# A gated S4 convolution and GLU kernel: products over 64 rows in three of its transform stages

## The chip, the cores and the metric

The kernel runs on one core of one Trainium2 chip. The core has five engines, each with its own instruction list that it works off in order: TensorE (PE, matrix products; its weight loads are shown apart as PEld), VectorE (DVE), ScalarE (ACT), GpSimd (POOL) and SyncE (SP), which here issues all DMA transfers. Transfers are carried out by 16 DMA engines. Engines wait for each other through semaphores. The metric is the time of one execution on the device in microseconds (us).

## The reference

Inputs are u of 2048 positions x 512 channels and the parameters of two branches. What is computed, cut to what matters:

```python
dt = exp(log_dt)[:, None]
P = exp((dt * A)[:, :, None] * l[None, None, :])      # A complex, 512 channels x 128 states
K = einsum("dn,dnl,dn->dl", Cc, P, dt * Bc).real      # one kernel of 2048 taps per channel
y = irfft(rfft(pad(u)) * rfft(pad(K)))[:L] + u * Dskip  # causal convolution per channel
b = (sigmoid(u @ w_gate) * (u @ w_up)) @ w_down       # GLU, inner width 1792
g = sigmoid((u * gate_w).sum(-1, keepdims=True))
out = g * y + (1 - g) * b
```

All inputs and outputs are fp32.

## The kernel before

**Two streams of work.** One stream is the GLU (`glu`), whose products use fp32 values split into a rounded high part and a low part (type fp32r): three products for each block of 128 rows, one pass of TensorE each. `hidden` (L416) makes 24 such products into the tiles `gups`, two PSUM buffers at a time out of a tag `gu` with three; the down projection (L367) adds 9 or 12 into `dps`. Altogether there are 1344 + 672 = 2016 GLU products of 128 x 128 x 512. The other stream is the convolution, done as a transform of length 2048 = 32 x 64 in plain fp32. An fp32 product leaves two records in the profile, since TensorE passes over it twice.

**The convolution's stages.**

- `rows` (L382): for each of 16 row blocks of u, the 32-point stage as two row-tiled products (each 64 rows of the array x 128 columns, at row positions 0 and 64, into two PSUM buffers), written to the DRAM tensor `a_u`.
- `kgen` (L192): for each of 16 groups of 32 channels, DVE builds powers by doubling (`double`, L181; three operations per step), TensorE forms K's taps (`kps`, L221: 64 products of 32 columns each), ACT copies them to `kst`, and TensorE applies the 32-point stage (L231): 16 products with all 128 rows of `kst` as weights and `wk` moving. `wk` has 128 columns; it is block diagonal, four blocks of 32 rows, so three quarters of it are zeros. ACT copies the results into `kev` (L235); after each four groups two transfers of 1 MB write it to `a_k`.
- `finish` (L251): for each of 16 q (two of the 32 frequencies k each) it loads the constants `w_in` and `wv` and the data `au` and `ak`, applies the 64-point stage to both (`stage2`, L243: column-tiled products of 64 columns at column positions 0 and 64), multiplies the spectra on DVE (L267, L268, four operations), and combines them to real part (L273) and imaginary part (L274). Three ACT copies of 64 partitions (L275 to L277) then move the parts so that each of the two k has its real part in partitions 0 to 63 and its imaginary part in 64 to 127. Two full products (L280, tile `ips`, one PSUM buffer, tag `kg`) do the inverse 64-point stage, ACT evicts them (L282), and each goes to the DRAM tensor `b_s`, laid out as [128 = (position, re/im)] x 32 k x 512.
- `final` (L313): for each of 16 row blocks m, one transfer of 512 KB brings `b_in` in, two column-tiled products with `wf` (128 rows x 64 columns, of which half are zeros) do the inverse 32-point stage, DVE adds the GLU's part (L322), and the result is written to `out`.

**What sets the order.** The program text interleaves the streams: `run_b(n)` advances the GLU by n units at each step of `kgen`, `finish` and `final` (ROW, MID, END, LAST set how much). From that text a planner makes, at build time, one fixed instruction list per engine: it takes instructions by priority as its own model says that their inputs and buffers are ready. `kgen`'s TensorE part runs at high priority. The chip then follows these lists whatever the real durations are. So an edit of one stage can move instructions of all others. A buffer is shared by all tiles of one tag; a tile waits until the one that had the buffer has been read for the last time. The tag `big` (three buffers of 512 KB) holds `au` and `ak` in `finish` and `b_in` in `final`; `fft` (two PSUM buffers) holds the outputs of L231, L247, L319 and L390; `o` (two buffers) the results on their way out. The pool `mid` (`rows`, `kgen`) is given up before the pool `end` (`finish`, `final`) is filled, so the first loads of `finish` follow the last `a_k` transfer.

**The stages' place in time.** `rows` and `kgen` come first, then `finish`, then, since every output row needs all 32 k, `final` behind the last write of `b_s`.

Of the kernel before, what the change touches and what calls it, by code (L numbers as in the profile page):

```python
# [25 lines left out]
OP = mybir.AluOpType  # L26
# [20 lines left out]
def constants():  # L47
# [5 lines left out]
    wk = np.zeros((4, 32, 2, 4, 32))  # L53
    wf = np.zeros((2, 2, 32, 2, 32))
    for j in range(2):
        for c in range(2):
            for jp in range(2):
                wu[jp, j, :, jp, c, j, :] = fwd[c]
            wf[j, c, :, j, :] = fwd[c].T / L
    for j in range(4):  # L60
        for c in range(2):
            wk[j, :, c, j, :] = fwd[c]
# [3 lines left out]
    for k in range(32):  # L66
# [6 lines left out]
    wv = wv.reshape(16, 2, P, P).transpose(0, 2, 1, 3)  # L73
# [3 lines left out]
        "c_wu": f(wu, P, 2, P), "c_wf": f(wf, P, 64), "c_wk": f(wk, P, 2, P),  # L77
# [5 lines left out]
def body(ctx, tc, xp, xt, prm, ldt, dsk, gw, wgu, wdn, c_wu, c_wf, c_wk, c_w2, c_wv, c_pw, out):  # L83
# [7 lines left out]
    b_s = dr.tile([P, 32, D], F32, name="b_s")  # L91
# [13 lines left out]
    wk = cst.tile([P, 2, P], F32, name="wk")  # L105
# [86 lines left out]
    def kgen(pp):  # L192
        nxt = bases(pp, 0)
        for gi in range(NG):
# [31 lines left out]
            kv = [k[:, :, 32 * s4:32 * s4 + 32].rearrange("p k (j s) -> p s j k", j=4) for k in kev]  # L226
            for s in range(0, 8, 4):
                p = fps()
                for i in range(4):
                    for c in range(2):  # L230
                        mm(p[64 * c:64 * c + 64, P * i:P * i + P], kst[:, s + i], wk[:, c], start=True, stop=True,  # L231
                           tile_position=(0, 64 * c), skip_group_check=True)
# [18 lines left out]
    def finish(pp):  # L251
        for q in range(16):
# [18 lines left out]

            y = pp.tile([P, 2, D], F32, name="y", bufs=2)
            nc.vector.tensor_tensor(y[:, 0], t1[:, 0], t1[:, 1], op=OP.subtract)  # L273
            nc.vector.tensor_tensor(t2[:, 0], t2[:, 0], t2[:, 1], op=OP.add)  # L274
            nc.scalar.activation(y[:64, 1], y[64:, 0], AF.Copy)  # L275
            nc.scalar.activation(y[64:, 1], t2[64:, 0], AF.Copy)
            nc.scalar.activation(y[64:, 0], t2[:64, 0], AF.Copy)  # L277
            for kb in range(2):
                p = ps.tile([P, D], F32, tag="kg", name="ips")
                mm(p, wv[:, kb], y[:, kb], start=True, stop=True)  # L280
                ev = pp.tile([P, D], F32, name="evb", bufs=3)
                nc.scalar.activation(ev, p, AF.Copy)  # L282
# [30 lines left out]
    def final(pp, wf, m):  # L313

        b = pp.tile([P, 2, D], F32, tag="big", bufs=3, name="b_in")
        nc.sync.dma_start(b, b_s[8 * m:8 * m + 8].rearrange("(j r) k d -> (r k) j d", j=2))
# [214 lines left out]
```

## Time and profile before

| | |
|---|---|
| median of the runs (758.28 to 763.95) | 760.19 us |
| the profiled execution, time | 766.59 us |
| its span | 764.7 us |
| granted TensorE clock, mean over the span | 0.966 |
| PE busy | 709.3 us (93%) |
| DVE busy | 622.5 us (81%) |
| ACT busy | 379.6 us (50%) |
| DMA, mean rate | 161 GB/s, 123.03 MB in all |
| first product of `finish` | at 572.5 us |
| last product of the inverse stage (L280) starts | at 714.9 us |
| first product of `final` (L319) | at 722.5 us |

Times inside the profile count from the start of the span. Busy time is the union of an engine's instructions; a matmul's end is modelled, so TensorE shown as busy is not TensorE at its peak. "gups<-xh,gu" reads: writes tile gups, reads xh and gu; "x32" counts records. A view of windows gives busy time in stretches; the chain gives the work that ended last, followed back from the end, each piece with its start and length; SPq rows are SP issuing a transfer or waiting to.

### The profile page before, as it was taken

Reading aid. Unit: us, or ns where it says so; the run is one execution under the profiler, and the core shown is the slowest. Engines: PE = TensorE matmul, PEld = TensorE weight load, DVE = VectorE, ACT = ScalarE, POOL = GpSimd, SP = SyncE. Lnnn points to the kernel's source line nnn. Section 1 sums busy time; section 2 is a strip of 40 time slices with the busy share of each in tenths; the row PEclk is TensorE's granted clock in tenths of the full one; section 3 lists DMA queues with packets and bytes.
Section 4 is the critical chain, followed back from the end, with each engine's and each line's share of the span. In section 5 each row is a group of like instructions: output and inputs, shape, how many; then the busy total and the mean of one; then the engine's idle time right before and its main releaser. Section 6 shows DMA issues by size and latency. Waiting matters only on the chain.

```text
span 764.7 us, 12698 instructions
## 1 busy us (share of the span) xinstructions
PE 709.3 (93%) x5024; PEld 478.7 (63%) x5024; DVE 622.5 (81%) x851; ACT 379.6 (50%) x624; POOL 3.6 (0%) x36
## 2 busy tenths in 40 slices
PE   5978869999999999999899998999999999999994
PEld 3445437787878778877687786877873333333640
DVE  5889796989998999998999898999927576477452
ACT  5264536381845446374565734637135655656310
POOL 0000000000000000000000000000000000000000
PEclk9789959999999999999999999999999999999998
DMA  6667652353134033655014330423167787876497
GB/s 230 185 201 215 171 158 77 128 188 132 63 110 140 34 132 109 220 172 188 12 34 157 122 150 8 138 96 99 56 244 255 266 264 240 266 249 227 143 308 249
DMA packets 63323, 123.03 MB, mean 161 GB/s; under 512 B 8480, under 2 KB 23072, under 8 KB 62240
## 3 DMA queue, kind: packets, MB, share of 16 engines
q1 hardware_dynamic: 63264, 122.23, 48.6%
q8 instruction: 39, 0.64, 0.3%
q14 instruction: 20, 0.16, 0.1%
HBM read 79.74 MB, written 42.47 MB: 160 GB/s over the span
## 4 chain that ended last, share of the span: by engine, by line
PE 44%; DVE 24%; ACT 14%; DMA 12%; issue 5%; SPq 1%; DVEq 0%; ACTq 0%
PE gups L424 13%; PE dps L367 11%; PE fps L247 8%; DVE T L189 5%; DVE T L190 5%; DVE tmp L188 4%; DMA wst<-wgu 4%; PE ips L280 4%; PE kps L221 3%; ACT L431 2%; PE fps L390 2%; DMA b_in<-b_s 2%; PE fps L231 2%; ACT gu L404 2%; DVE h L432 2%
## 5 line engine op out<-in xcount | busy, mean ns | idle before, releaser
L424 PE MATMUL gups<-xh,gu 128*128 128x512 f32 x896 | 294.5, 404 | 12.7 <-ACT gu L404 10.3
L424 PEld LDWEIGHTS gups<-xh,gu 128*128 128x128 f32 x896 | 170.6, 192 | 66.0 <-issue 12.9
L424 PE MATMUL gups<-xl,gu 128*128 128x512 f32 x448 | 181.3, 405 | 0.0
L367 PE MATMUL dps<-dnw,hh 128*128 128x512 f32 x448 | 152.9, 406 | 11.2 <-ACT hh L433 11.2
L188 DVE TENSOR_TENSOR tmp<-T,bz 128x64 f32<-128x64 f32 (+2 forms) x96 | 114.8, 1196 | 2.4
L190 DVE TENSOR_TENSOR T<-T,tmp 128x64 f32<-128x64 f32 (+2 forms) x96 | 114.7, 1195 | 0.8
L367 PEld LDWEIGHTS dps<-dnw,hh 128*128 128x128 f32 x448 | 84.3, 191 | 49.6 <-ACT hh L433 16.9
L189 DVE TENSOR_TENSOR T<-T,bz 128x64 f32<-128x64 f32 (+2 forms) x96 | 114.7, 1195 | 0.0
L424 PEld LDWEIGHTS gups<-xl,gu 128*128 128x128 f32 x448 | 86.2, 192 | 28.2 <-issue 10.5
L367 PE MATMUL dps<-dnw,hl 128*128 128x512 f32 x224 | 90.1, 404 | 2.1 <-DVE hl L434 1.3
L433 ACT ACTIVATE hh<-h 128x512 fp32r<-128x512 f32 x56 | 35.1, 628 | 70.1 <-DVE h L432 70.1
L431 ACT ACTIVATE sg<-gups 128x512 f32<-128x512 f32 x56 | 33.4, 596 | 50.5 <-PE gups L424 50.1
L367 PEld LDWEIGHTS dps<-dnw,hl 128*128 128x128 f32 x224 | 42.9, 192 | 15.8 <-issue 4.2
L432 DVE TENSOR_TENSOR h<-gups,sg 128x512 f32<-128x512 f32 x56 | 38.2, 685 | 16.9 <-PE gups L424 14.3
L404 ACT ACTIVATE gu<-wst 128x1024 fp32r<-128x1024 f32 x28 | 29.6, 1058 | 41.8 <-DMA wst<-wgu 29.2
L267 DVE TENSOR_TENSOR t<-fps,uf 128x512 f32<-128x512 f32 x32 | 22.0, 687 | 31.2 <-PE fps L247 19.8
L434 DVE TENSOR_TENSOR hl<-h,hh 128x512 fp32r<-128x512 f32 x56 | 38.4, 687 | 9.4 <-ACT hh L433 9.2
L247 PE MATMUL fps<-ak,w_in 128*64 128x512 f32 x128 | 42.1, 610 | 0.1
L235 ACT ACTIVATE kev<-fps 128x256 f32<-128x256 f32 x64 | 33.7, 675 | 15.3 <-PE fps L231 15.3
L247 PE MATMUL fps<-au,w_in 128*64 128x512 f32 x128 | 38.4, 610 | 1.9 <-DVE ud L301 0.8
L373 DVE TENSOR_TENSOR acc<-acc,dps 128x512 f32<-128x512 f32 x48 | 32.2, 682 | 7.8 <-PE dps L367 7.7
L221 PEld LDWEIGHTS kps<-T 128*32 128x32 f32 x2048 | 31.6, 115 | 8.8 <-issue 8.8
(84 smaller groups left out, 691.1 us busy)
## 6 DMA issues: line engine op xcount, KB each, us to landing
wst<-wgu SPq DMA_DIRECT2D x28, 512.0 KB, 4.4
a_u<-evu SPq DMA_DIRECT2D x32, 256.0 KB, 3.3
a_k<-kev SPq DMA_DIRECT2D x8, 1024.0 KB, 6.1
au<-a_u SPq DMA_DIRECT2D x16, 512.0 KB, 5.6
ak<-a_k SPq DMA_DIRECT2D x16, 512.0 KB, 5.0
b_s<-evb SPq DMA_DIRECT2D x32, 256.0 KB, 2.5
b_in<-b_s SPq DMA_DIRECT2D x16, 512.0 KB, 4.7
wsd<-wdn SPq DMA_DIRECT2D x28, 256.0 KB, 3.3
```

The source lines that it names most:

```text
L188: nc.vector.tensor_tensor(t2, src, sb, op=OP.mult)
L189: nc.vector.tensor_tensor(dst, src, br, op=OP.mult)
L190: nc.vector.tensor_tensor(dst, dst, t2[:, :, ::-1], op=OP.add)
L221: mm(p[32 * j:32 * j + 32, s].rearrange("p (a b) -> p a b", a=2), T[:, 0, ch, c], T[:, 1:3, ch, c], start=(c == 0), stop=(c == 1), tile_po ...
L247: mm(p[64 * kb:64 * kb + 64], w[:, kb, 64 * c:64 * c + 64], a(kb), start=True, stop=True, tile_position=(0, 64 * kb), skip_group_check=True)
L367: mm(p, a[:, hs], dnw[:, b], start=(n == 0), stop=(n == last))
L404: nc.scalar.activation(gu[:, 0], s4, AF.Copy)
L424: mm(p, gu[:, a, k, dc], b[:, dc], start=(n == 0), stop=(n == 11))
L431: nc.scalar.activation(sg, pp[0], AF.Sigmoid)
L432: nc.vector.tensor_tensor(h, pp[1], sg, op=OP.mult)
L433: nc.scalar.activation(hh, h, AF.Copy)
L434: nc.vector.tensor_tensor(hl, h, hh.bitcast(F32), op=OP.subtract)
```

## The change

Three stages are rewritten, and the DRAM layout between two of them.

- **K's first stage.** The constant `wk` keeps two of its four blocks (64 columns). The 128 rows of `kst` are taken as two halves of 64 rows; each of 8 s x 2 halves x 2 parts (re, im) is a product of 64 rows x 64 columns at one of four tile positions, 64 columns moving. 32 products per group replace 16; both PSUM buffers of `fft` are taken at once, one per half.
- **The inverse 64-point stage.** `y` keeps real and imaginary parts where DVE leaves them (the imaginary part is written to `y[:, 1]`). The three ACT copies go. Each k is one half of the rows; its result is the sum of two products of 64 rows (re, then im) accumulated in its own PSUM buffer, one of tag `kg` and one of tag `gu`. Four products replace two.
- **The last stage.** `b_s` becomes [64 positions][32 k][2 parts][512]. `final` runs once per pair of row blocks (called at odd m). It takes two `big` buffers, each filled by two transfers of 256 KB, one per row block into its own half of the partitions. Eight products of 64 rows x 32 columns fill two PSUM buffers, one per row block; `wf` loses its zeros. Then come both results and both writes.

```diff
-            kv = [k[:, :, 32 * s4:32 * s4 + 32].rearrange("p k (j s) -> p s j k", j=4) for k in kev]
-            for s in range(0, 8, 4):
-                p = fps()
-                for i in range(4):
+            ph = [fps(), fps()]
+            for s in range(8):
+                for jh in range(2):
+                    r = slice(64 * jh, 64 * jh + 64)
                     for c in range(2):
-                        mm(p[64 * c:64 * c + 64, P * i:P * i + P], kst[:, s + i], wk[:, c], start=True, stop=True,
-                           tile_position=(0, 64 * c), skip_group_check=True)
-                p4 = p.rearrange("p (s j k) -> p s j k", s=4, j=4)
+                        mm(ph[jh][64 * c:64 * c + 64, 64 * s:64 * s + 64], kst[r, s], wk[r, c], start=True, stop=True,
+                           tile_position=(64 * jh, 64 * c), skip_group_check=True)
+            for jh in range(2):
+                p4 = ph[jh].rearrange("p (s j k) -> p s j k", s=8, j=2)
                 for i in range(2):
-                    nc.scalar.activation(kv[i][:, s:s + 4], p4[:, :, :, 16 * i:16 * i + 16], AF.Copy)
+                    kv = kev[i][:, :, 32 * s4 + 16 * jh:32 * s4 + 16 * jh + 16].rearrange("p k (j s) -> p s j k", j=2)
+                    nc.scalar.activation(kv, p4[:, :, :, 16 * i:16 * i + 16], AF.Copy)
...
-            nc.vector.tensor_tensor(t2[:, 0], t2[:, 0], t2[:, 1], op=OP.add)
-            nc.scalar.activation(y[:64, 1], y[64:, 0], AF.Copy)
-            nc.scalar.activation(y[64:, 1], t2[64:, 0], AF.Copy)
-            nc.scalar.activation(y[64:, 0], t2[:64, 0], AF.Copy)
+            nc.vector.tensor_tensor(y[:, 1], t2[:, 0], t2[:, 1], op=OP.add)
+
+            pi = [ps.tile([P, D], F32, tag="kg", name="ips"), ps.tile([P, D], F32, tag="gu", bufs=3, name="ips")]
+            for c in range(2):
+                for kb in range(2):
+                    r = slice(64 * kb, 64 * kb + 64)
+                    mm(pi[kb], wv[r, c], y[r, c], start=(c == 0), stop=(c == 1), tile_position=(64 * kb, 0))
             for kb in range(2):
-                p = ps.tile([P, D], F32, tag="kg", name="ips")
-                mm(p, wv[:, kb], y[:, kb], start=True, stop=True)
                 ev = pp.tile([P, D], F32, name="evb", bufs=3)
-                nc.scalar.activation(ev, p, AF.Copy)
+                nc.scalar.activation(ev, pi[kb], AF.Copy)
                 nc.sync.dma_start(b_s[:, 2 * q + kb], ev)
...
-        b = pp.tile([P, 2, D], F32, tag="big", bufs=3, name="b_in")
-        nc.sync.dma_start(b, b_s[8 * m:8 * m + 8].rearrange("(j r) k d -> (r k) j d", j=2))
-        p = fps()
-        for j in range(2):
-            mm(p[64 * j:64 * j + 64], wf, b[:, j], start=True, stop=True, tile_position=(0, 64 * j),
-               skip_group_check=True)
-        o = pp.tile([P, D], F32, tag="o", bufs=2, name="o")
-        nc.vector.scalar_tensor_tensor(o, p, g[:, m:m + 1], accs[m], op0=OP.mult, op1=OP.add)
-        nc.sync.dma_start(out[m], o)
+        ph = [fps(), fps()]
+        for h in range(2):
+            b = pp.tile([P, 2, D], F32, tag="big", bufs=3, name="b_in")
+            for jb in range(2):
+                l2 = 4 * (m + jb) + 2 * h
+                nc.sync.dma_start(b[64 * jb:64 * jb + 64], b_s[l2:l2 + 2].rearrange("x k c d -> (k c) x d"))
+            for x in range(2):
+                for jb in range(2):
+                    r, o = slice(64 * jb, 64 * jb + 64), 64 * h + 32 * x
+                    mm(ph[jb][o:o + 32], wf[r], b[r, x], start=True, stop=True, tile_position=(64 * jb, o),
+                       skip_group_check=True)
+        for jb in range(2):
+            o = pp.tile([P, D], F32, tag="o", bufs=2, name="o")
+            nc.vector.scalar_tensor_tensor(o, ph[jb], g[:, m + jb:m + jb + 1], accs[m + jb], op0=OP.mult, op1=OP.add)
+            nc.sync.dma_start(out[m + jb], o)
...
-            final(pp, wf, m)
+            if m % 2:
+                final(pp, wf, m - 1)
             run_b(LAST * left)
```

The constants follow (`wk` with 64 moving columns, `wf` with 32, `wv` in the order of parts and halves), and `b_s` is declared as `[64, 32, 2, D]`.

More of the change, by code (lines that the diff above doesn't have):

```diff
@@ L52, in constants @@
     wu = np.zeros((2, 2, 32, 2, 2, 2, 32))
-    wk = np.zeros((4, 32, 2, 4, 32))
-    wf = np.zeros((2, 2, 32, 2, 32))
+    wk = np.zeros((2, 2, 32, 2, 2, 32))
+    wf = np.tile(fwd.transpose(2, 0, 1), (2, 1, 1, 1)) / L
     for j in range(2):
@@ L58, in constants @@
                 wu[jp, j, :, jp, c, j, :] = fwd[c]
[L59 to L62, printed above, removed]
+            wk[:, j, :, c, j, :] = fwd[c]
     l2, k2 = np.arange(64)[:, None], np.arange(64)[None, :]
@@ L90, in body @@
     a_k = dr.tile([NQ, P, 32, P], F32, name="a_k")
-    b_s = dr.tile([P, 32, D], F32, name="b_s")
+    b_s = dr.tile([64, 32, 2, D], F32, name="b_s")
     dts = dr.tile([16, 32], F32, name="dts")
```

8 lines of the change are left out of this document (4 added, 4 removed).

## The prediction

> **What bounds the kernel now.** I read four views: busy time by windows, the chain that ended last, SP's own timeline, and the groups by shape.
>
> ```profile
> 200.00:300.00 100.00, 98.58 (x852) 80.42 (x841) 96.31 (x124) 50.57 (x78) 0.65 (x6) 1.00 0.31 108
> 300.00:400.00 100.00, 96.20 (x835) 77.62 (x835) 92.34 (x116) 56.37 (x89) 0.63 (x6) 0.98 0.37 124
> 650.00:700.00 50.00, 50.00 (x156) 16.66 (x155) 30.86 (x55) 28.84 (x54) 0.00 (x0) 1.00 0.79 256
> 745.00:750.00 5.00, 2.16 (x8) 0.46 (x8) 2.13 (x4) 0.00 (x0) 0.00 (x0) 1.00 0.96 324
> 750.00:755.00 5.00, 1.54 (x4) 0.54 (x6) 0.95 (x2) 0.00 (x0) 0.00 (x0) 0.81 0.93 322
> ```
>
> After the window come busy us of PE, weight loads, DVE, ACT and POOL, then clock, DMA share and GB/s. There are three stages. While K is generated, DVE is busy 92 to 96%; PE's 96 to 98% there flatters it, because ends are modelled. In `finish` PE never pauses and DVE is at 62%. At the end PE is below half and the DMA engines are 93 to 96% busy. So a PE gain is worth little in the first stage, all of itself in the second, and nothing in the third. The chain gives the borders and the durations:
>
> ```profile
> 555.33 1.90 PE fps L231 x32
> 557.22 5.67 PE gups L424 x24
> 562.89 8.45 PE dps L367 x36
> 571.34 0.68 PE gups L424 x3
> ...
> 572.47 3.83 PE fps L247 x16
> ...
> 714.56 0.90 PE ips L280 x2
> ...
> 716.10 2.49 DMA b_s<-evb
> ...
> 718.66 3.65 DMA b_in<-b_s
> ...
> 722.45 1.08 PE fps L319 x4
> 723.53 0.89 PE gups L424 x3
> 724.42 1.01 PE fps L319 x4
> ...
> 742.80 3.56 DMA b_in<-b_s
> ```
>
> One GLU product (L424, L367) costs 8.45/36 = 0.235 us. The last K stage ends at 557.2. The first `finish` product starts at 572.5, because a_k has to be written and au and ak loaded first; 63 GLU products fill that hole. The last inverse product ends at 715.5, so `finish` takes 143.0 us. The first `final` product starts 7.0 us later, the last GLU product ends at 742.8, and the rest up to 764.7, 21.9 us, is transfers.
>
> **The change, part by part.** Prices first.
>
> ```profile
> 46.70 1.11 PE fps L390 x4
> 622.15 1.87 PE fps L247 x8
> 650.68 1.01 PE fps L247 x4
> 654.02 0.86 PE ips L280 x2
> 584.06 0.69 DVE t L267
> ...
> 587.14 0.61 DVE t2f L274
> ```
>
> Each fp32 product leaves two records. Two column tiles run side by side: four records take 1.01, eight 1.87. So a pair of products, a **slot**, is 0.86 us, the same as one full product (0.86). Row tiles do so too: the L390 pair, two 64-row products into two banks, takes 1.11 for four records. Each change between a tiled shape and any other costs about 0.2: 1.01 less 0.86 behind the pair, and in the rows above three GLU products take 0.89 where three times 0.235 is 0.71.
>
> The Trainium skill, "TensorEngine Tiling (Array Packing)", Key Properties, says that a change of tiling mode drains TensorE; by it every alternation of `final` and GLU products pays, and the sum stays as it is. The trace agrees with its 0.2 us.
>
> *K's first stage.*
>
> ```profile
> L231 PE MATMUL fps<-wk,kst 128*64 128x128 f32 x512 | 33.7, 285 | 3.3 <-DVE evu L392 1.9 <-ACT evu L391 0.7 <-issue 0.6
> PE gups L424 13%; PE dps L367 11%; PE fps L247 8%; DVE T L189 5%; DVE T L190 5%; DVE tmp L188 4%; DMA wst<-wgu 4%; PE ips L280 4%; PE kps L221 3%; ACT L431 2%; PE fps L390 2%; DMA b_in<-b_s 2%; PE fps L231 2%; ACT gu L404 2%; DVE h L432 2%
> ```
>
> Now 32 records of 128 columns take 1.90 us per group; then 64 records of 64 columns on four tiles. The trace shows row pairs and column pairs, not both together: at best 0.95, at worst still 1.90. L231 is 2% of the chain, 15 us, so the most that halving can return is 7.5. DVE is at 92 to 96% here and gets almost nothing less to do; I take half, **-4 us**, bounds -7.5 and +3 (a new order of the same work).
>
> *Where GLU work goes.* This is not in the diff; the order of the built program shows it. PE's list, cut at the three borders (products; the four middle rows describe `finish`):
>
> ```
>                                    before  after
> GLU products up to the last K stage  1740   1711
> GLU between it and the first au        63     11
> GLU within finish                     138    186
> fp32 slots within finish              108    107
> changes of tiled shape there           83     89
> GLU behind the last inverse product    75    108
> ```
>
> The hole of 15.3 us stays, since the a_k write and the loads make it, but is filled with 2.6 us of PE work where there were 14.8. What is missing comes back in the two stages where it costs.
>
> *finish.* Before: 138 x 0.235 + 108 x 0.86 + 83 x 0.2 = 141.9, against 143.0 in the trace, so counting is fair. After: 186 x 0.235 + 107 x 0.86 + 89 x 0.2 = 153.5. The four half products of an inverse make two slots, as two full ones did: packing returns nothing by itself. The three ACT copies per q go:
>
> ```profile
> L275 ACT ACTIVATE y<-y 64x512 f32<-64x512 f32 x16 | 10.1, 629 | 6.9 <-DVE y L273 6.7
> L262 ACT ACTIVATE uf<-fps 128x512 f32<-128x512 f32 x32 | 18.6, 594 | 24.0 <-PE fps L247 20.6 <-DMA rst<-acc 3.1
> L322 DVE SCALAR_TENSOR_TENSOR o<-fps,g,rst 128x512 f32<-128x512 f32 x8 | 6.0, 749 | 4.5 <-PE fps L319 3.7 <-DMA out<-o 0.8
> ```
>
> That is 30 us off ACT, which is busy 29 of 50 us there and hidden behind PE: nothing. The new order adds a wait: the inverse of q now stands directly behind the ak products of the same q, with at most a few products between, while before half of it was spread into the next q. Behind the waiting product PE queues the next q's products and GLU work. With zero at the end of the first ak pair, the six DVE steps (0.6 each, 584.06 to 587.75) free the second bank at 2.8; the next q's second au half runs to 3.65, the inverse 3.8 to 5.5, then au and ak to 7.4. PE's own work in that loop is 6 x 0.86 + 3 x 0.2 = 5.8: 1.6 us idle. Five of the sixteen q have no GLU product in the loop: 8 us. So finish takes 161.5, **+18.5**. Bounds: +10.5 with no idle time; +29 if DVE's side work (gate, rest, acc) holds each q up by one more step.
>
> *final.* SP's queue and the transfers:
>
> ```profile
> 742.80 1.63 SPq L316 DMA_DIRECT2D b_in<-b_s  x2
> 746.04 1.01 SPq L323 DMA_DIRECT2D out<-o  x2
> 747.14 1.00 SPq L316 DMA_DIRECT2D b_in<-b_s  x2
> 750.32 1.01 SPq L323 DMA_DIRECT2D out<-o  x2
> 751.42 4.41 SPq L316 DMA_DIRECT2D b_in<-b_s  x2
> a_u<-evu SPq DMA_DIRECT2D x32, 256.0 KB, 3.3
> b_s<-evb SPq DMA_DIRECT2D x32, 256.0 KB, 2.5
> b_in<-b_s SPq DMA_DIRECT2D x16, 512.0 KB, 4.7
> out<-o SPq DMA_DIRECT2D x16, 256.0 KB, 3.4
> ```
>
> While GLU work is left, the final products stand two by two between GLU products in both programs, so eight half-width ones cannot fill the array at once. Before, eight such places: 8 x 1.21 + 46 x 0.235 = 20.5 (trace: 722.45 to 742.80). After, thirteen places and 79 GLU products behind the first: 13 x 1.21 + 79 x 0.235 = 34.3, **+13.9**. By then only three and a bit of eight pairs of row blocks are done.
>
> The other pairs go round SP. Before, two row blocks take 4.3 us (742.80, 747.14, 751.42): loads stand ahead of the writes, two or three buffers deep. After, a pair needs two of the three `big` buffers, and SP's list reads: out of pair p, first half; one load; out of p, second half; two loads for the second buffer of p+1; one for p+2. So those two loads are issued only when p's last result exists. From p's first result: 1.4 us until they are issued (0.35 per out, 0.75 for the second result by L322), 3.3 to land (the 64-partition transfer a_u in the list), 1.15 for products, 0.75 for the result, 0.2 of handshakes: 6.8 per pair against 4.3. Four pairs, 3.2 us ahead (742.80 to 746.04) and 3.5 behind: 33.9 against 21.9, **+12.0**. Bounds for both parts: +16 if the loop still runs at 4.3, +31 at 8 us.
>
> The Trainium skill, "DMA: Bandwidth & Descriptors", Rules for kernel authors, says that two transfers to the two partition halves serialize and that one over 128 partitions is better. By it the halved loads would cost as much as the whole ones and a little more, and the loop stays near 6.8. The trace leans that way: a_u on 64 partitions takes 3.3 us and b_s on 128, of the same 256 KB, 2.5.
>
> **Sum.** -4 + 18.5 + 13.9 + 12.0 = +40.4 us. The profiled execution has a span of 764.7 and a time of 766.6; it would become 807. It lies 6.4 above the median of 760.2, so the median becomes **801**.
>
> **The rivals.**
>
> 1. *The tail stays a matter of bandwidth.* If the loads run ahead after all, four pairs take 17 us and not 27, and finish shows little idle time: -4 + 13 + 16 = +25, 785. For it: 0.93 to 0.96 DMA share with the same bytes. Against: SP issues in order. Chance 0.20.
> 2. *Faster: PE's slots decide and GLU work is free to move.* If K's stage really holds up DVE (L231 in the chain) and returns its 7.5, `final` halves its slots (16 to 8, -6.9), and the hole and the order cost nothing because the removed copies (three of 0.63 us per q) were what delayed finish: 760 - 14 = 746. Its point: the first au must start 12 us earlier than 572 to cancel the emptier hole. Against: DVE's 92 to 96%, ACT at 58% in finish. Chance 0.04.
> 3. *The row tiles don't run side by side* when they accumulate two products each: 16 x 2 x 0.86 = 27.5 more, 828. Against: the L390 row, though its pairs don't accumulate. Chance 0.05.
> 4. *No change within 1%* (about what a measurement of this kernel can tell): the hole is filled by other means and the tail hides in transfers, 762. Chance 0.04.
>
> The forecast has 0.67. **Range:** low ends -7.5 + 10.5 + 16 = +19 give 779, high ends +3 + 29 + 31 = +63 give 823; reaching to rival 1 and leaving out rivals 2 and 4 and part of 3, 776 to 820. Faster by over 1% 0.04, within 1% 0.04, slower by over 1% 0.92.
>
> **What would show it.** In the profile after: PE idle for some 12 us just ahead of the first au product, which starts near 565 to 570; the last inverse product near 725 to 732 instead of 715.5; GLU products until some 41 us behind it instead of 27; then outs on SP at intervals of 6 to 7 us per pair, with the DMA share of that stretch near 0.65 instead of 0.95; ACT's y copies gone without a trace in the chain. A K stage of 64 records taking 1.9 would refute four tiles at once. I am wrong if the first au starts before 560, if finish takes 143 or less, or if the pairs at the end follow each other in 4.3 us.

## The result, and the profile after

The changed kernel takes 810.99 us (median of 4 runs, 805.92 to 816.40), the kernel before 761.72 us beside it: ratio 1.0641, 95% interval 1.0592 to 1.069. The profiled execution took 812.28 us with a span of 810.4, which is 45.7 more than the 764.7 of before. The forecast was 801 (776 to 820).

The chain of the kernel after shows the borders of the stages (start, length, what):

```profile
538.18 0.66 PE fps L228 x33
539.13 0.69 PE fps L228 x31
541.92 5.89 DMA a_k<-kev
549.70 5.02 DMA au<-a_u
554.86 5.40 PE fps L246 x12
...
604.21 1.92 PE ips L278 x8
...
721.40 2.04 PE ips L278 x8
...
727.21 3.65 DMA b_in<-b_s
...
730.99 1.05 PE fps L323 x4
...
763.27 1.36 PE dps L372 x5
...
769.28 4.94 DMA b_in<-b_s
...
774.26 1.94 PE fps L323 x4
...
788.52 5.73 DMA b_in<-b_s
```

K's last stage product ends at 539.8 (before 557.2), the first au product starts at 554.9 (572.5), the last inverse product ends at 723.4 (715.4), the first `final` product starts at 731.0 (722.5), and the last GLU product ends at 764.6 (743.0). Set against before, stage by stage:

| | before | after | difference | predicted |
|---|---|---|---|---|
| to the end of K's first stage | 557.2 | 539.8 | -17.4 | -4 |
| hole up to the first au product | 15.2 | 15.0 | -0.2 | 0 |
| `finish`, to the last inverse product | 143.0 | 168.5 | +25.5 | +18.5 |
| to the first `final` product | 7.1 | 7.6 | +0.5 | 0 |
| from there to the last GLU product | 20.5 | 33.6 | +13.1 | +13.9 |
| from there to the end | 21.7 | 45.8 | +24.1 | +12.0 |

(The forecast counted the last two rows as 20.5 and 21.9.) Every change of more than 1 us goes the way that was forecast, but three sizes are off, and two of the errors cancel: K's stage gave 13 us more than expected, and the pairs at the end took 12 more.

Windows of the kernel after (busy us of PE, weight loads, DVE, ACT, POOL, then granted clock, DMA share, GB/s):

```profile
540.00:555.00 15.00, 2.98 (x13) 1.83 (x14) 0.69 (x1) 1.90 (x4) 0.00 (x0) 0.72 0.65 239
555.00:565.00 10.00, 9.38 (x28) 2.63 (x30) 6.83 (x13) 3.06 (x9) 0.00 (x0) 0.73 0.95 324
...
575.00:600.00 25.00, 22.55 (x82) 11.04 (x80) 14.43 (x26) 9.90 (x22) 0.00 (x0) 0.93 0.56 188
600.00:723.00 123.00, 119.16 (x430) 44.64 (x428) 68.78 (x120) 35.63 (x76) 0.00 (x0) 1.00 0.59 196
...
765.00:810.00 45.00, 27.96 (x76) 3.30 (x72) 8.51 (x12) 0.72 (x1) 0.00 (x0) 0.58 0.53 153
```

TensorE stands still ahead of 555: 3.0 us of work in 15. Then its clock is at 0.73 for 10 us. In the tail the DMA engines are at 53% and 153 GB/s, where the kernel before had 76% and 264 GB/s from 743 to 764, its own tail: the new tail is a loop of waits, not a matter of bandwidth.

### The profile page after: what moved, and what is told of

Same layout as the page of the kernel before. It is cut to its first block, busy times and chain, and to the rows that moved or that the text cites. A ratio compares the mean times of both kernels' runs of the same rounds, so it can differ in the third digit from the quotient of the medians.

```text
span 810.4 us, 13994 instructions
## 1 busy us (share of the span) xinstructions
PE 728.1 (90%) x5664; PEld 468.1 (58%) x5664; DVE 623.1 (77%) x851; ACT 348.6 (43%) x575; POOL 3.7 (0%) x36
## 4 chain that ended last, share of the span: by engine, by line
PE 42%; DVE 31%; DMA 9%; ACT 9%; issue 7%; SPq 2%; DVEq 0%; ACTq 0%
PE gups L429 13%; PE dps L372 11%; PE fps L246 8%; DVE T L187 6%; DVE T L186 6%; DVE tmp L185 6%; PE ips L278 3%; DMA b_in<-b_s 3%; PE fps L323 3%; DVE h L437 3%; PE kps L218 2%; PE fps L395 2%; DVE hl L439 2%; DVE gu L412 1%; DMA wsd<-wdn 1%
## 5 line engine op out<-in xcount | busy, mean ns | idle before, releaser
L429 PE MATMUL gups<-xh,gu 128*128 128x512 f32 x896 | 291.4, 401 | 11.5 <-ACT gu L409 11.2
L429 PE MATMUL gups<-xl,gu 128*128 128x512 f32 x448 | 178.4, 399 | 0.0
L372 PE MATMUL dps<-dnw,hh 128*128 128x512 f32 x448 | 154.7, 406 | 17.6 <-ACT hh L438 15.7
L246 PE MATMUL fps<-au,w_in 128*64 128x512 f32 x128 | 52.0, 649 | 15.5 <-DMA au<-a_u 11.9
L323 PE MATMUL fps<-b_in,wf 64*32 64x512 f32 x128 | 42.1, 809 | 14.6 <-DMA b_in<-b_s 14.4
L372 PEld LDWEIGHTS dps<-dnw,hl 128*128 128x128 f32 x224 | 42.5, 190 | 21.5 <-DVE hl L439 6.3
L261 ACT ACTIVATE uf<-fps 128x512 f32<-128x512 f32 x32 | 19.1, 596 | 70.5 <-PE fps L246 47.2
L246 PE MATMUL fps<-ak,w_in 128*64 128x512 f32 x128 | 46.4, 639 | 0.0
L234 ACT ACTIVATE kev<-fps 128x256 f32<-128x256 f32 x64 | 33.6, 682 | 13.2 <-PE fps L228 13.2
```

The source lines that it names most:

```text
L234: nc.scalar.activation(kv, p4[:, :, :, 16 * i:16 * i + 16], AF.Copy)
L246: mm(p[64 * kb:64 * kb + 64], w[:, kb, 64 * c:64 * c + 64], a(kb), start=True, stop=True, tile_position=(0, 64 * kb), skip_group_check=True)
L323: mm(ph[jb][o:o + 32], wf[r], b[r, x], start=True, stop=True, tile_position=(64 * jb, o), skip_group_check=True)
L372: mm(p, a[:, hs], dnw[:, b], start=(n == 0), stop=(n == last))
L429: mm(p, gu[:, a, k, dc], b[:, dc], start=(n == 0), stop=(n == 11))
```

## The experiments

Each version was measured in 4 to 12 executions beside the kernel before; "ratio" is its time over that of the kernel before in the same measurement. The table has the borders of every profiled execution, in us, and the measured times. A minus in the column "GLU behind" means that the GLU ended before the last stage began.

| run | K's end | hole | finish | to final | GLU behind | rest | span | median | ratio (95%) |
|---|---|---|---|---|---|---|---|---|---|
| before | 557.2 | 15.2 | 143.0 | 7.1 | 20.5 | 21.7 | 764.7 | 761.72 | |
| after | 539.8 | 15.0 | 168.5 | 7.6 | 33.6 | 45.8 | 810.4 | 810.99 | 1.0641 (1.0592 to 1.069) |
| k_only | 541.2 | 15.5 | 148.6 | 6.6 | 24.7 | 16.9 | 753.6 | 756.25 | 0.9933 (0.9899 to 0.9967) |
| inv_only | 556.7 | 14.2 | 167.3 | 7.3 | 28.4 | 19.3 | 793.2 | 792.05 | 1.0395 (1.0355 to 1.0435) |
| last_only | 555.1 | 14.8 | 142.1 | 6.9 | 20.1 | 56.3 | 795.3 | 797.03 | 1.0456 (1.0412 to 1.05) |
| no_last | 537.6 | 15.1 | 167.9 | 7.4 | 28.4 | 18.6 | 775.0 | 779.61 | 1.0227 (1.0179 to 1.0275) |
| last_out_on_act | 550.0 | 14.7 | 142.6 | 6.9 | 22.5 | 34.8 | 771.6 | 776.99 | 1.0189 (1.0116 to 1.0263) |
| last_128_parts | 553.7 | 14.8 | 143.5 | 7.6 | 20.3 | 22.9 | 762.9 | 763.84 | 0.9998 (0.9967 to 1.0029) |
| inv_other_banks | 553.7 | 14.7 | 156.1 | 8.1 | -3.8 | 48.3 | 777.0 | 773.38 | 1.0122 (1.0065 to 1.018) |
| k_inv_other_banks | 541.1 | 16.0 | 155.7 | 7.3 | -0.5 | 41.9 | 761.5 | 763.08 | 0.9978 (0.9946 to 1.0009) |
| k_products_twice | 546.1 | 36.0 | 158.1 | 6.9 | 26.5 | 19.1 | 792.7 | 795.23 | 1.041 (1.0316 to 1.0504) |
| k_inv_own_bank | 550.6 | 16.4 | 145.1 | 7.2 | 27.8 | 19.1 | 766.1 | 770.28 | 1.0103 (1.0057 to 1.0149) |
| k_inv_swap | 541.4 | 16.2 | 151.2 | 7.3 | -0.9 | 40.8 | 756.0 | 758.37 | 0.9911 (0.9874 to 0.9947) |
| all_three_mended | 539.6 | 15.7 | 149.1 | 7.7 | -1.4 | 44.6 | 755.3 | 757.63 | 0.9925 (0.9895 to 0.9955) |

One profile is one execution, and its borders have a spread of their own. `before`, `last_only`, `last_out_on_act` and `last_128_parts` have the same instructions in the same order on TensorE, VectorE and ScalarE up to the first `final` product, and yet K's stage ends at 557.2, 555.1, 550.0 and 553.7 in them, while finish differs by 1.4 us at most. So a difference in the column "K's end" is safe only where it is clear of these 7 us.

### Each part alone

The theory to begin with is the forecast's: K's stage gives little, the inverse moves GLU work and adds a wait, the last stage turns into a loop round SyncE's list. Each run takes one part of the change, or two, into the kernel before. `k_only` is K's first stage:

```diff
-    wk = cst.tile([P, 2, P], F32, name="wk")
+    wk = cst.tile([P, 2, 64], F32, name="wk")
...
-                        mm(p[64 * c:64 * c + 64, P * i:P * i + P], kst[:, s + i], wk[:, c], start=True, stop=True,
-                           tile_position=(0, 64 * c), skip_group_check=True)
+                        mm(ph[jh][64 * c:64 * c + 64, 64 * s:64 * s + 64], kst[r, s], wk[r, c], start=True, stop=True,
+                           tile_position=(64 * jh, 64 * c), skip_group_check=True)
```

> Only K's first stage is changed; inverse and last stage as before. In the built order 1719 GLU products stand ahead of the last K stage (1740 before, 1711 after), 65 in the hole, finish counts 149.5 us (141.9), tail 90 GLU products. Theory A, the 17 us by which K's stage ended earlier in the changed kernel come from the shorter products themselves: last K stage ends near 542, finish 5 to 8 us longer, tail 4 longer, 752 in all. Rival B, DVE sets the pace and the 17 us came from GLU products moved out of the stage and from a luckier order: it ends at 550 to 555 and the whole is 760 to 766.

It takes 0.9933 of the time before, 5 us less. In the profiles K's stage ends at 541.2, 16 us earlier, and 10 of these are given back: finish +5.6, GLU behind the first `final` product +4.2. The 16 is a high reading: the six profiles with the old stage end it at 550.0 to 557.2 (mean 554.4), the six with the new one (all but `k_inv_own_bank` and `k_products_twice`, which change this stage further) at 537.6 to 541.4 (mean 540.1). That is 14 us between the means, and the two groups don't overlap. (The spans of the two profiles differ by 11 us and the medians by 5, since the profiled execution of before lay 5 us above the median.) Why finish grows can be counted with the forecast's prices: in the built order it holds 142 GLU products, 112 slots and 99 changes of shape, 142 x 0.235 + 112 x 0.86 + 99 x 0.2 = 149.5, against 148.6 measured. In that order 21 GLU products fewer stand ahead of the end of K's stage, 4.9 us of the 16.

`inv_only` is the row-tiled inverse, in the old layout of `b_s`:

```diff
-            nc.scalar.activation(y[:64, 1], y[64:, 0], AF.Copy)
...
+            pi = [ps.tile([P, D], F32, tag="kg", name="ips"), ps.tile([P, D], F32, tag="gu", bufs=3, name="ips")]
...
+                    mm(pi[kb], wv[r, c], y[r, c], start=(c == 0), stop=(c == 1), tile_position=(64 * kb, 0))
```

> Only the inverse stage is changed. Built order: 1720 GLU products, 2 in the hole, finish and what stands behind it product for product as in the changed kernel up to the first final product (186 in finish, 108 behind). Theory A, the inverse stage alone empties the hole and lengthens finish: finish near 167, GLU products until 31 us after the first final product, then the last stage of before, 785 to 795. Rival B, an inverse without copies is neutral and the loss belongs to the combination: within 1% of 761.

It brings 24.3 us in finish by itself and 7.9 behind it. `last_only` is the new layout of `b_s` with the paired `final`:

```diff
-    b_s = dr.tile([P, 32, D], F32, name="b_s")
+    b_s = dr.tile([64, 32, 2, D], F32, name="b_s")
...
-            final(pp, wf, m)
+            if m % 2:
+                final(pp, wf, m - 1)
```

> Only the last stage is changed; up to the first final product every list is that of before. Theory A, loads that wait for results on SP: pairs follow each other in 9 to 10 us as in the changed kernel, six of them after the last GLU product, 33 to 38 us more: 795 to 799. Rival B, the pairs were slow in the changed kernel because GLU work stood among them and transfers would overlap otherwise: pairs at 5 to 7 us, 770 to 780.

Everything ahead of the last GLU product is as before, and all of the loss is behind it: 56.3 us instead of 21.7. `no_last` takes K's stage and the inverse together and leaves `final` as it was:

```diff
+    wk = cst.tile([P, 2, 64], F32, name="wk")
...
+            pi = [ps.tile([P, D], F32, tag="kg", name="ips"), ps.tile([P, D], F32, tag="gu", bufs=3, name="ips")]
```

> The changed kernel with the last stage of before (its lists up to the first final product are the changed kernel's). Theory A, the last stage's structure costs what the tail of the changed kernel is longer than 22 us: last GLU product 31 us after the first final product, then about 22: 781 to 785. Rival B, the tail is long because 108 GLU products stand in it: 800 to 808.

Its finish (167.9) is that of `inv_only`. So the loss has two separate sources, the inverse and the last stage, and K's stage is a gain.

### What makes the last stage slow

The forecast says that a pair's later loads stand behind the writes of the pair before. In `last_out_on_act` the writes leave that list; the loads of 64 partitions and the two-by-two products stay:

```diff
-            nc.sync.dma_start(out[m + jb], o)
+            nc.scalar.dma_start(out[m + jb], o)
```

> The kernel before with the packed last stage alone; its output writes go out from ScalarE's queue instead of SyncE's. The 64-partition loads, the two-by-two products and the one eviction to a pair stay as in last_only (795.3 profiled, 56.3 us behind the last GLU product). Theory A (in last_only a pair's load stands behind the writes of the pair before in SyncE's list, so that load, product, eviction and write follow one another): with the writes gone from that list the loads run ahead again, the stretch behind the last GLU product falls to 20 to 30 us, and the time is 760 to 778 us. Rival (loads of 64 partitions and products at half the clock are slow by themselves): the stretch stays at 45 us or more, 785 to 797 us.

In `last_128_parts` the writes stay where they were, but `b_s` has an order in which one transfer fills 128 partitions with half a pair:

```diff
-    b_s = dr.tile([64, 32, 2, D], F32, name="b_s")
+    b_s = dr.tile([32, 32, 2, 2, D], F32, name="b_s")
...
-            for jb in range(2):
-                l2 = 4 * (m + jb) + 2 * h
-                nc.sync.dma_start(b[64 * jb:64 * jb + 64], b_s[l2:l2 + 2].rearrange("x k c d -> (k c) x d"))
+            g2 = 2 * m + 2 * h
+            nc.sync.dma_start(b, b_s[g2:g2 + 2].rearrange("j k c x d -> (j k c) x d"))
```

> The kernel before with the packed last stage alone, but the scratch of the inverse's results is laid out so that one load fills all 128 partitions with a pair's half (512 KB to a load, and half as many loads); the writes stay on SyncE's queue, and the inverse's output columns are permuted to suit. Theory A (what costs is a load that waits in SyncE's list behind a write): the list still has writes between the loads, but a load is a whole half of a pair, so two pairs are under way at a time; the stretch behind the last GLU product is 25 to 40 us, and the time 765 to 780 us. Rival B (the cost is in the loads of 64 partitions): 20 to 24 us and 758 to 764 us, as before the change. Rival C (two-by-two products and one eviction to a pair are slow by themselves): 50 us or more, 790 to 797 us.

SyncE's own timeline, first of the kernel after:

```profile
777.00 0.34 SPq L328 DMA_DIRECT2D out<-o  x1
777.39 0.57 SPq L319 DMA_DIRECT2D b_in<-b_s  x1
778.07 0.55 SPq L328 DMA_DIRECT2D out<-o  x1
778.71 1.94 SPq L319 DMA_DIRECT2D b_in<-b_s  x3
786.81 0.34 SPq L328 DMA_DIRECT2D out<-o  x1
```

One write, one load, one write, three loads, as the forecast read from the list; the loads at 778.71 stand behind the second result, and the next result comes only at 786.8, 9.8 us after the first. Then of `last_out_on_act`, and of `last_128_parts`:

```profile
735.92 27.17 SPq L319 DMA_DIRECT2D b_in<-b_s  x18
```

```profile
745.03 2.31 SPq L319 DMA_DIRECT2D b_in<-b_s  x2
748.96 0.99 SPq L328 DMA_DIRECT2D out<-o  x2
750.05 1.08 SPq L319 DMA_DIRECT2D b_in<-b_s  x2
753.99 6.35 SPq L328 DMA_DIRECT2D out<-o  x4
```

With the writes away, 18 loads follow one another and the stretch behind the GLU falls from 56.3 to 34.8: 21.5 of its 34.6 extra us are the order of SyncE's list. The time is in theory A's range, the stretch 5 us above it. What is left, 13 us, has other causes than the place of the writes in that list. In `last_128_parts` the stretch is 22.9 and the whole time that of before (rival B's 758 to 764), although the writes are back between the loads; but there are half as many loads, two to each stop, so that the two mends overlap. The groups of DMA issues name a likely cause of the rest (KB each, median us from issue to landing); the first row is the kernel after, the second `last_128_parts`:

```profile
b_in<-b_s SPq DMA_DIRECT2D x32, 256.0 KB, 4.5
```

```profile
b_in<-b_s SPq DMA_DIRECT2D x16, 512.0 KB, 4.9
```

Half the bytes into half the partitions take nearly as long as all of them into all. Whether that is due to the halved partitions or to the halved size, no run tells apart: other loads of 256 KB in the kernel before, over 128 partitions, took 3.3 us (`wsd`) to 5.1 us (`ud`). How the 13 us divide between these transfers, the products behind them (granted clock 0.50 from 745 to 765 in `last_out_on_act`) and results that wait for an earlier write (two waits of 4 us in its chain, one before), these runs can't say. Rival C, products two by two as the fault, falls: `last_128_parts` has the same products.

### What makes the inverse slow

Row tiles go to separate accumulators, so the change needs two where one was enough; it took the second from `gu`, the GLU's. The Trainium skill, "TensorEngine Tiling (Array Packing)", Restrictions and Gotchas, says that different row tiles write to different PSUM banks. No run here put two row tiles into one bank. The buffers of a tag are handed out in the order of the program text. So `hidden` products that the text places behind an inverse can't be put ahead of it. A first sign is in the chains around the hole: `no_last`, and then `k_only`, which differs from it by the inverse alone.

```profile
539.70 5.88 DMA a_k<-kev
...
547.94 4.78 DMA ak<-a_k
```

```profile
542.54 9.09 PE gups L424 x40
551.63 4.78 PE dps L367 x20
556.70 1.94 PE fps L247 x8
```

The hole has the same length, 15 us; in `k_only` GLU products fill it, in `no_last` TensorE waits for transfers. `inv_other_banks` and, with K's stage, `k_inv_other_banks` change only where the second accumulator comes from:

```diff
-            pi = [ps.tile([P, D], F32, tag="kg", name="ips"), ps.tile([P, D], F32, tag="gu", bufs=3, name="ips")]
+            pi = [ps.tile([P, D], F32, tag="kg", name="ips"), fps()]
```

> The kernel before with the row-tiled inverse alone, as inv_only (793.2 profiled), but the inverse's second accumulator comes from the pool of the transforms' accumulators (fft) instead of the GLU's (gu). In the built order 63 GLU products then stand in the hole before the first au transform instead of 2, and the stage after it has 195 GLU products, 96 four-way slots and 51 switches of tile mode. Theory A (the change's 25 us in this stage come from sharing the GLU's accumulators, which puts GLU products behind inverses that have not run): from the first au transform to the last inverse 137 to 150 us instead of 167, the GLU ends 10 to 22 us behind the first product of the last stage instead of 28, and the time is 747 to 765 us. Rival (the row-tiled inverse, whose two products per accumulator wait for two evictions, is slow by itself): the stage stays at 160 us or more, and the time at 780 us or more.

> The packed first stage of K and the row-tiled inverse together, the last stage as before, as no_last (775.0 profiled), with the inverse's second accumulator from the pool of the transforms (fft). In the built order 65 GLU products stand in the hole, and behind it 203 GLU products, 96 slots and 55 switches. Theory A (shared accumulators were the fault): K's last first-stage product ends near 541 as in no_last, the hole is 15, the finish 140 to 152 instead of 168, the GLU ends 8 to 20 us behind the first product of the last stage; the time is 738 to 757 us, under both kernels. Rival (row-tiled inverse slow by itself): the finish 160 or more, 768 us or more.

The hole is full again, no GLU work is left when `final` begins, and the times fall from 792.05 to 773.38 and from 779.61 to 763.08. But finish takes 156 us where theory A had 137 to 152, and both times are 6 to 8 us above its range. The chain of `k_inv_other_banks` repeats one turn every 8.94 us:

```profile
668.27 0.43 issue
668.70 0.60 ACT evb L282
669.34 2.85 PE fps L247 x12
672.20 2.95 PE gups L424 x12
675.15 0.62 PE ips L279
```

The last transforms now wait for an eviction, since the inverse took a buffer of `fft`; and ACT evicts the other result first. `k_inv_swap` turns that order round:

```diff
-            for kb in range(2):
+            for kb in (1, 0):
                 ev = pp.tile([P, D], F32, name="evb", bufs=3)
```

> k_inv_other_banks (761.5 profiled, 155.7 from the first au transform to the last inverse) with one change: of the two results of an inverse, the one in the transforms' accumulator is evicted first, the other second. Theory A (each of 16 turns waits for two evictions of 0.6 us before the next transform may have its accumulator): one eviction less in each turn, 16 x 0.6 = 9.6 us at most, 146 to 151 us for the stage, 750 to 756 us in all. Rival (the turn is set by VectorE's six operations and the inverse behind them): the stage stays at 154 us or more and the time at 760 to 764 us.

```profile
666.20 3.66 PE fps L247 x16
669.86 2.95 PE gups L424 x12
672.80 0.62 PE ips L279
```

Now 16 transform records follow in a row and the eviction is out of the chain there. A turn, from one inverse to the next, falls from 8.94 (666.21 to 675.15) to 8.52 (664.28 to 672.80); ten of the 15 turns are of this kind, which makes 4 us. Finish falls by 4.5 to 151.2, just above the 146 to 151 of theory A, and the whole to 758.37, 2 us above its range and 0.9911 of before. `k_inv_own_bank` gives the inverse two accumulators of the tag `kg`, which it shares with K's taps of the stage ahead, and takes one away from the GLU's down product:

```diff
-            p = ps.tile([P, 8, 64], F32, tag="kg", name="kps")
+            p = ps.tile([P, 8, 64], F32, tag="kg", bufs=2, name="kps")
...
-            pi = [ps.tile([P, D], F32, tag="kg", name="ips"), ps.tile([P, D], F32, tag="gu", bufs=3, name="ips")]
+            pi = [ps.tile([P, D], F32, tag="kg", bufs=2, name="ips") for _ in range(2)]
...
-                        p = ps.tile([P, D], F32, tag="dn", bufs=2, name="dps")
+                        p = ps.tile([P, D], F32, tag="dn", bufs=1, name="dps")
```

> K's packed first stage and the row-tiled inverse together as in no_last (775.0 profiled), but the inverse has two accumulators of its own (kg), and the GLU's down product has one instead of two. In the built order 1733 GLU products come before the end of K's first stage, 65 in the hole, 113 in the stage behind it with 111 slots and 112 switches, 105 behind the last inverse. Theory A (the inverse costs because it shares accumulators with GLU or transforms): no wait in it but for its own data, 541 to 546 to the end of K's stage, 143 to 152 for the stage behind the hole, 20 to 26 us of GLU behind the first product of the last stage; 750 to 760 us, the same as k_only within 1%. Rival R (the row-tiled form is slow by itself): 155 us or more in that stage, over 766 us. Rival S (one accumulator for the down product is too few): the end of K's stage at 550 us or later.

Finish takes 145.1, against a count of 113 x 0.235 + 111 x 0.86 + 112 x 0.2 = 144.4. So the row-tiled form isn't what makes finish 168 (rival R falls), and it isn't fast either: 145.1 stands against 143.0 with the copies and the full products, although the count has 25 GLU products fewer (5.9 us); 29 more changes of shape (5.8 us) and three more slots (2.6 us) take their place. But K's stage ends at 550.6 instead of 541 (rival S). One reason is that the down product, now with one accumulator, waits for its sum to be read; another that 14 more GLU products stand ahead of that end than in `k_only`, 3.3 us. The waits of TensorE up to 550.6 (us in all, times, longest) show the first; neither row is among the seven largest of `k_only`:

```profile
PE dps L367 <- DVE acc L373: 4.5, 6, 1.0
...
PE dps L367 <- ACT acc L371: 2.6, 4, 0.7
```

So the total of 770.28 is not theory A's 750 to 760: an accumulator that the inverse gets is missing elsewhere, in every place that was tried.

### Why K's stage gives 14 to 16 us

The products themselves got shorter. In the timelines of before and of the kernel after, a group of K's first stage looks like this:

```profile
236.62 1.97 PE L231 MATMUL fps<-wk,kst 128*64 128x128 f32 x32
```

```profile
226.32 1.16 PE L228 MATMUL fps<-wk,kst 64*64 64x64 f32 x64
```

In `k_only` most groups save these 0.8 us, and the 16 together some 10.5 us. VectorE was read as the bound there, so that shorter products should return almost nothing. `k_products_twice` takes `k_only` and issues each of these products twice, into the same place:

```diff
-                        mm(ph[jh][64 * c:64 * c + 64, 64 * s:64 * s + 64], kst[r, s], wk[r, c], start=True, stop=True,
-                           tile_position=(64 * jh, 64 * c), skip_group_check=True)
+                        for _ in range(2):
+                            mm(ph[jh][64 * c:64 * c + 64, 64 * s:64 * s + 64], kst[r, s], wk[r, c], start=True,
+                               stop=True, tile_position=(64 * jh, 64 * c), skip_group_check=True)
```

> k_only with every product of K's first stage issued twice into the same place (1024 more products, the same evictions; the results are the same). In the built order 160 fewer GLU products stand before the last of K's first-stage products (1559 instead of 1719), 157 instead of 65 in the hole, 208 instead of 142 in the stage behind it. Theory P (the middle is paid for on TensorE: each product there costs its own length, about 0.021 us for a 64x64 one and 0.245 us for a GLU product, whatever VectorE does): 541.2 + 21 - 39 = 523 us for the end of K's first stage, the hole not under 30 us, and the whole 21 us above k_only, 772 to 782 us. Theory D (VectorE's chain of T sets the end of K's stage, and products hide under it): the end stays at 536 to 545 us and the whole at 756 us, or, as the GLU products moved are late, above 790.

Theory P falls: 160 GLU products, some 39 us of TensorE work, were moved out of the stage, 21 us of K products added, and its end came at 546.1, not at 523. Theory D has the end within 1 us of its range and the whole time right, above 790. But it says that the products hide, and the end is 4.9 us later than in `k_only`, which is less than the 7 us that one list moves by. Clearer than the border are the waits. The window up to the end of K's stage, for before, `k_only` and `k_products_twice`:

```profile
0.00:557.20 557.20, 516.70 (x4365) 398.19 (x4365) 502.65 (x649) 286.69 (x445) 3.62 (x36) 0.96 0.40 128
```

```profile
0.00:541.20 541.20, 496.42 (x4856) 380.31 (x4856) 501.24 (x646) 284.09 (x441) 3.66 (x36) 0.97 0.41 132
```

```profile
0.00:546.10 546.10, 486.88 (x5720) 376.33 (x5720) 494.22 (x632) 278.93 (x430) 3.66 (x36) 0.95 0.39 125
```

VectorE's work (third number) is the same in before and `k_only`, 502.7 and 501.2. What shrinks is its idle time: 54.6 us, then 40.0; with the products doubled it is 51.9. The waits of VectorE in the same stretch, largest first (us in all, times, longest), name the part that is K's:

```profile
DVE T L201 <- PE kps L221: 11.4, 8, 3.3
DVE hl L434 <- ACT hh L433: 6.5, 6, 1.8
```

```profile
DVE T L199 <- PE kps L219: 6.2, 9, 1.6
```

```profile
DVE T L199 <- PE kps L219: 12.9, 10, 3.4
```

VectorE writes the next T only when TensorE has read the last one for K's taps, and these products wait in TensorE's list behind whatever stands there. 11.4 us of such waits become 6.2, and 12.9 with the products doubled. That is 5 of the 14.6 us; others that shrink belong to the GLU (hl behind ACT: 6.5 before, 2.4 in `k_only`). Over all profiles the change is smaller but as clear: 9.3 to 11.7 us of T behind K's taps in the six with the old stage, 6.2 to 8.4 in the six with the new one. How much of those comes from the shorter products and how much from the new order of the same instructions stays open, since no run changed the one without the other.

### The whole change with both faults mended

`all_three_mended` joins `k_inv_swap` and the last stage of `last_128_parts`.

```diff
+            pi = [ps.tile([P, D], F32, tag="kg", name="ips"), fps()]
...
+            for kb in (1, 0):
...
+    b_s = dr.tile([32, 32, 2, 2, D], F32, name="b_s")
```

> All three parts of the change, with the two faults found mended: k_inv_swap (756.0 profiled, 40.8 us behind the last GLU product, in which only the last stage runs) plus the last stage of last_128_parts (packed products, one load of 128 partitions to a half pair). Theory A (what made the change slow is the inverse's accumulator and the waiting loads, not the products): 541 for the end of K's stage, 149 to 153 for the stage behind the hole, and behind it a last stage that is set by its bytes as in k_inv_swap, so 752 to 762 us, not slower than before. Rival (packed products at half the clock set the last stage where no GLU product runs beside it): the stretch behind the last inverse at 56 us or more instead of 47, and 765 us or more.

757.63 us, 0.9925 (0.9895 to 0.9955) of before: theory A, with finish at 149.1. The stretch behind the last inverse is 51.0 us, between the 47 of `k_inv_swap` and the 56 of the rival, so in these two profiles the packed last stage takes some 4 us more there. The three parts, which cost 49 us as they were put, gain 5.6. `k_only` (0.9933) and `k_inv_swap` (0.9911) lie within its interval, so nothing measured here shows a gain from the inverse or from the last stage; what gains is K's stage. These three are the versions that beat both kernels, each by less than 1% of before.

## Why the prediction was right or wrong, point by point

The total was right within its range, the 810.99 lying 10 us above the forecast, and its likeliest case is what happened. That the total came this close is in part luck: K's stage came out 13 us better than forecast, finish and the pairs at the end 7 and 12 us worse. Of its signs, the idle TensorE ahead of the first au product (11.9 us) and the GLU products until 41 us behind the last inverse came; the first au product, the last inverse (723.4 instead of 725 to 732), the interval of the pairs (9.8 instead of 6 to 7) and the DMA share (0.53 instead of 0.65) missed. By its own steps:

- **K's first stage: wrong in size.** "DVE is at 92 to 96% here and gets almost nothing less to do; I take half" gave -4 with a bound of -7.5 from the chain's share; it was -17.4, -16 in `k_only`, and -14 between the means of the two groups of six profiles. 4 to 8% of 557 us is room for more than 7.5, and VectorE stood idle for 54.6 us. A line's share of the chain is not a bound on what shortening it returns when it stands in an in-order list between two engines that wait for each other. The four tiles do run at once: 64 records in 0.66 + 0.69 us with a gap of 0.3 between, and in 1.16 where nothing stands between, where 1.90 would have refuted it.
- **The first au near 565 to 570: wrong**, it is at 554.9, from the same step. The forecast named a start ahead of 560 as a sign of being wrong, and it was, for that step; rival 2's point (12 us ahead of 572) was passed too. Neither made the kernel faster, because the other parts of rival 2 didn't come.
- **The hole: right.** It has the same length and is empty. The cause was found by the experiments, not by the forecast, which only read the order: the inverse's second accumulator out of `gu`.
- **finish: right in kind, 7 us short** (+25.5 against +18.5, inside its bounds). The loop that was forecast is there: where a turn holds no GLU product, it takes 7.5 us (7.4 forecast), and the transform waits in it for VectorE's last read of its buffer:

```profile
652.07 1.92 PE ips L278 x8
...
657.82 0.61 DVE t2f L267
...
658.57 1.04 PE fps L246 x2
659.61 0.62 PE ips L278
```

  Two terms were missing. One is the clock: 0.73 in the first 10 us behind the idle hole and 0.93 in the 25 us up to 600 cost some 2.7 + 1.8 us, by these windows. The Trainium skill, "TensorE: Matmul & The Clock Gate", HAM oscillation, says that an idle gap over about 3.4 us lowers it. The trace agrees, with 11.9 us idle ahead. The other is a single wait of TensorE, for the GLU's down product:

```profile
PE dps L372 <- ACT hh L438: 2.4, 1, 2.4
```

  Together these make 6.9 of the 7 us. The inverse itself was priced rightly: its eight records take 1.92 us, two slots and one change of shape.
- **The removed copies return nothing, packing returns nothing: right.** `k_inv_own_bank` has finish at 145.1, its count by slots and changes at 144.4.
- **GLU behind the first `final` product: right**, +13.1 against +13.9. Order and prices by count hold.
- **The pairs at the end: the mechanism right, the price wrong.** A pair takes 9.8 us (777.00 to 786.81), not 6.8, and four of them give the missing 12. The terms that were mis-sized: landing 4.9 to 5.7 us instead of 3.3, products 1.94 instead of 1.15, issue 1.7 instead of 1.4. The 3.3 came from a transfer of another stage, and a write; the products ran in gaps, with the granted clock at 0.58 in that stretch, where the same four records took 0.98 us at full clock. The rule of the Trainium skill on the halves ("DMA: Bandwidth & Descriptors", Rules for kernel authors), quoted in the forecast, would have put a half near the whole. The trace leans that way, with 4.5 us for 256 KB and 4.9 for 512.
- **Rivals.** 1 (bandwidth): no, 0.53 of DMA share. 3 (row tiles don't run side by side): no, an inverse takes 1.92 us, not 3.4. 4: no.

## What to carry to other kernels

When an edit takes one more buffer out of a pool, ask who shares the pool and in what order it is handed out: here the tag alone (`gu` or `fft`) was worth 16 to 19 us. When loads and writes share one in-order queue, write the list down and look for a load that waits behind a result; and look before you split a load in two, since here a load of half the size took nearly as long. A part that gains can hide in a change that loses: K's stage alone is the gain, and only taking the parts one by one shows it. And compare a border between two profiles only when you know how far it moves between profiles of the same lists: here 7 us of 557.

## What the runs showed of the hardware that was not expected

- 64 records on tiles of 64 rows x 64 columns, 64 columns moving, take 1.16 us on four tile positions, 18 ns each; 32 records on tiles of 128 x 64, 128 columns moving, took 1.97 us on two, 62 ns each.
- An idle hole costs twice: in the kernel after, the first 12 transform records behind it take 5.40 us at a granted clock of 0.50, where before 16 took 3.83 at 1.00.
- A load of 256 KB into 64 partitions takes 4.5 us in the last stage, one of 512 KB into 128 partitions 4.9.
